# T5-bias attention followed by a three-way maxout FFN on one core: transposes moved to the PSUM banks of the attention sums, q and k loaded two batches ahead, the bias band mirrored by VectorE

## The chip, the cores and the metric

The kernel runs on one core of a Trainium2 chip (trn2). The metric is device time in microseconds (us), as the median of repeated runs. TensorE (PE) does the matrix products and transposes, VectorE (DVE) and ScalarE (ACT) read the results out of PSUM and do the elementwise work, GpSimd (POOL) issues the loads that also convert from float32 to bfloat16, and SyncE (SP) issues the plain transfers.

## The reference

Eight batches of eight heads, 576 positions, 64 numbers a head. The bias depends only on the distance between the positions, and is constant from a distance of 128 on.

```
scores = q @ k^T / 8 + bias_table[bucket(|i - j|)]
attn   = softmax(scores)
x      = (attn @ v), heads side by side          # 4608 x 512
h      = max(max(x @ w1, x @ w2), x @ w3)        # 4608 x 768
out    = h @ w_out                               # 4608 x 512
```

## The kernel before, in words

The attention runs over 32 pairs of heads: four pairs (`hp`) in each of eight batches (`b`). For a pair, q and k are transposed on TensorE (`transpose_q`, `transpose_k`, lines 333 and 343): five 128-column transposes each into one PSUM bank, then one VectorE copy to SBUF (lines 340 and 350). The scores are made with the keys on the partitions and 288 queries (`c` = 0 or 1) on the free axis. First come the scores of the last 64 keys (`et`), then four key tiles for `c` = 0 and four for `c` = 1 (`e`). Each score tile takes two PSUM banks of a pool of two such tiles, ScalarE takes the exponential (line 371), and VectorE multiplies the part near the diagonal with the exponential of the bias (lines 376 and 383, from the tiles `bandt` and `band`).

`attend` (line 394) then sums over the keys: `den` (the softmax denominator, by ones) and `o` (attention times v), with one PSUM bank each (pool `ps_a`, one buffer for each tag). ScalarE makes 1/den as exp(-ln den), and VectorE multiplies and writes `xT`, the input of the FFN. The attend steps run late: that of the previous pair's second half after the first two score tiles of `c` = 0, that of this pair's first half after the first two of `c` = 1. In the first two pairs (`keep` = 2) up to two of them are held back.

The FFN is cut into nine chunks of 512 tokens. A chunk has 72 matmuls of stage 1 (18 groups of four, each group in one bank, read out in turn by ScalarE, line 282, and VectorE, lines 285 and 288) and 24 of stage 2 (four groups of six, copied out by line 311 or 313 and stored). These 96 matmuls wait in the list `pending`. `fill(n)` issues about n of them at five places in a pair, by `RATES`; what the list doesn't hold is not carried over. A chunk enters the list when the batch that completes its tokens is done, so the first four pairs have no FFN work, and the last two chunks run after the last pair.

Before the change the transposes of the next pair take their bank from the pool `ps_f` (two banks, tag `ff`), which the FFN groups use too. `transpose_q` stands after `fill` in the first half of `c` = 0, `transpose_k` after `fill` in the second half.

TensorE runs all matmuls and transposes in the order of the program. For the other engines the builder settles the order by the dependences and its own plan; each engine works through its queue in order and waits at an instruction whose input is not there.

At the start `make_band` (line 245) builds the bias factors. A table `w_sb` of 511 exponentials for each head, symmetric about its middle, is written to DRAM and read back so that each partition has a window shifted by one (`hank`). TensorE then reverses the partitions by a product with the mirrored identity `jrev`, and VectorE copies the result from PSUM into `band`, and part of it into `bandt`. The lines that the change touches are 179 to 199 (identity, `jrev`), 212 to 225 (`w_sb`), 245 to 250 (`make_band`), 333 to 351 (transposes), 419 (`RATES`) and 424 to 461 (the loop).

Of the kernel before, what the change touches and what calls it, by code (L numbers as in the profile page):

```python
# [10 lines left out]
F32 = mybir.dt.float32  # L11
BF16 = mybir.dt.bfloat16
ALU = mybir.AluOpType
# [26 lines left out]
def kernel(  # L40
# [12 lines left out]
    nc = tc.nc  # L53
    B, H, S, D = q.shape
    d_model, d_ff = moe_w1.shape
    NB = bias_table.shape[0]
    P = 128
    assert d_model == H * D and S == 576 and D == 64 and NB == 32 and H == 8
    inv_sqrt_d = 1.0 / float(np.sqrt(D))
    HP = H // 2  # L60
# [5 lines left out]
    CH = 512  # L66
    NCH = NTOK // CH
    BAND = 3 * P
    HALF = 2 * P - 1
    WL = 2 * HALF + 1  # L70

    const = ctx.enter_context(tc.tile_pool(name="const", bufs=1))
# [16 lines left out]
    def mm(*args, **kw):  # L89
        tc.keep_in_program_order(nc.tensor.matmul(*args, **kw))  # L90
# [36 lines left out]
    def load_q(b, h0, h1, tiles):  # L127
        load_main(q, b, h0, h1, tiles[0])
        nc.gpsimd.dma_start(
            out=qtail[b % 2][0:64, h0:h1, :], in_=q[b, h0:h1, KT * P : S, :].rearrange("h p d -> p h d"),  # L130
        )

    def load_k(b, h0, h1, tiles):
        load_main(k, b, h0, h1, tiles[1])
        load_tail(k, b, h0, h1, ktail)
# [31 lines left out]
    def load_tiles():  # L167
        q_sb = loads.tile([P, KT, H, D], BF16, tag="q_sb", name="q_sb")
        k_sb = loads.tile([P, KT, H, D], BF16, tag="k_sb", name="k_sb")
        v_sb = loads.tile([P, KT, H, D], BF16, tag="v_sb", name="v_sb")  # L170
        return q_sb, k_sb, v_sb

    batch = [None] * B
# [2 lines left out]
    load_k32(2, 4)  # L176
    load_q(0, 0, 2, batch[0])

    ident_f = stage.tile([P, P], F32, name="ident_f")
    make_identity(nc, ident_f[:])  # L180
    ident = const.tile([P, P], BF16, name="ident")
    nc.vector.tensor_copy(ident[:], ident_f[:])  # L182
    load_v(0, 0, 2, batch[0])
    load_q(0, 2, H, batch[0])
    jrev_f = stage.tile([P, P], F32, name="jrev_f")
    nc.gpsimd.memset(jrev_f[:], 0.0)
    nc.gpsimd.affine_select(
        out=jrev_f[:], in_=jrev_f[:], compare_op=ALU.not_equal, fill=1.0,
        base=-(P - 1), pattern=[[1, P]], channel_multiplier=1,
    )  # L190
    jrev = const.tile([P, P], BF16, name="jrev")
    nc.vector.tensor_copy(jrev[:], jrev_f[:])
    load_v(0, 2, H, batch[0])
    ones = const.tile([P, 64], BF16, name="ones")
    nc.vector.memset(ones[:], 1.0)
# [15 lines left out]
    while ranges[single] == (single, single + 1):  # L211
        single += 1
    nc.vector.tensor_copy(w_sb[:, HALF : HALF + single], etab[:, 0:single])
    for vv, rg in enumerate(ranges):
        if rg is None or vv == NB - 1:
            continue
        lo, hi = rg
        assert hi <= P
        segs = [(HALF + lo, HALF + hi)] if vv >= single else []
        if lo > 0:  # L220
            segs.append((HALF - hi + 1, HALF - lo + 1))
        for m0, m1 in segs:
            nc.vector.tensor_copy(  # L223
                w_sb[:, m0:m1], etab[:, vv : vv + 1].to_broadcast([H, m1 - m0])
            )
# [16 lines left out]
    cast_k32(2, 4, batch[0][1])  # L242
    cast_k32(4, H, batch[0][1])

    def make_band(hp):
        for par in range(2):
            pb = ps_f.tile([P, CH], F32, tag="ff", name="pb")
            mm(pb[:, 0:BAND], lhsT=jrev[:], rhs=hank[:, 2 * hp + par, :])
            nc.vector.tensor_copy(band[hp][:, par, :], pb[:, 0:BAND])
            nc.vector.tensor_copy(bandt[hp][64 * par : 64 * par + 64, :], band[hp][0:64, par, 0:192])  # L250

    w_bf = []
    for wi, wk in enumerate((moe_w1, moe_w2, moe_w3)):
        wb = const.tile([P, DCH, d_ff], BF16, name=f"w{wi}_bf")
# [71 lines left out]
    def fill(mms):  # L326
        budget[0] = budget[0] + mms if pending else 0.0
        while pending and budget[0] >= 0.5:
            budget[0] -= 1
            pending.pop(0)()  # L330


    def transpose_q(b, hp):
        hs = slice(2 * hp, 2 * hp + 2)
        tq = ps_f.tile([P, 2 * CH], BF16, tag="ff", name="tq")
        for t in range(KT):
            tr(tq[:, P * t : P * t + P], batch[b][0][:, t, hs, :].rearrange("p h d -> p (h d)"), ident[:])
        tr(tq[:, KT * P : KT * P + P], qtail[b % 2][:, hs, :].rearrange("p h d -> p (h d)"), ident[:])
        qT = qkt.tile([P, S], BF16, tag="qT", name="qT")
        nc.vector.tensor_copy(qT[:], tq[:, 0:S])  # L340
        return qT

    def transpose_k(b, hp):
        hs = slice(2 * hp, 2 * hp + 2)
        tk = ps_f.tile([P, 2 * CH], BF16, tag="ff", name="tk")
        for t in range(KT):
            tr(tk[:, P * t : P * t + P], batch[b][1][:, t, hs, :].rearrange("p h d -> p (h d)"), ident[:])
        tr(tk[:, KT * P : KT * P + P], ktail[b % 2][:, hp, :], ident[:])
        kT = qkt.tile([P, (KT + 1) * P], BF16, tag="kT", name="kT")
        nc.vector.tensor_copy(kT[:], tk[:, 0 : (KT + 1) * P])  # L350
        return kT

    def scores(hp, qT, kT, c, t):

        sc = ps_s.tile([P, 2, CH], F32, tag="sc", name="sc")
        if c is None:
            for cc in range(2):
                mm(  # L360
                    sc[:, cc, 0:QC], lhsT=kT[:, KT * P : KT * P + P], rhs=qT[:, cc * QC : cc * QC + QC]
                )
            e = etp.tile([P, 2, QC], BF16, tag="et", name="et")
        else:
            for par in range(2):
                r = slice(64 * par, 64 * par + 64)
                mm(
                    sc[:, par, 0:QC], lhsT=kT[r, P * t : P * t + P], rhs=qT[r, c * QC : c * QC + QC]
                )
            e = ep.tile([P, 2, QC], BF16, tag="e", name="e")  # L370
        nc.scalar.activation(out=e[:], in_=sc[:, :, 0:QC], func=ACTF.Exp, scale=inv_sqrt_d)  # L371

        def factor():
            if c is None:
                lo = KT * P - P - QC
                nc.vector.tensor_tensor(
                    out=e[:, 1, lo:QC], in0=e[:, 1, lo:QC], in1=bandt[hp][:], op=ALU.mult
                )
            else:
                lo = max(P * t - P, c * QC)  # L380
                hi = min(P * t + 2 * P, c * QC + QC)
                if hi > lo:
                    nc.vector.tensor_tensor(  # L383
                        out=e[:, :, lo - c * QC : hi - c * QC], in0=e[:, :, lo - c * QC : hi - c * QC],
                        in1=band[hp][:, :, lo - P * t + P : hi - P * t + P], op=ALU.mult,
                    )

        if made:
            factor()
        else:  # L390
            factors.append(factor)
        return e
# [23 lines left out]
        nc.vector.tensor_tensor(out=xT[hp][:, x0 : x0 + QC], in0=o[:, 0:QC], in1=rd[:], op=ALU.mult)  # L416

    ready = {n: (n * CH + CH - 1) // S for n in range(NCH)}
    RATES = (6.0, 2.5, 7.0, 4.0, 4.0)
    pairs = [(b, hp) for b in range(B) for hp in range(HP)]  # L420
    late = []
    made, factors = [], []
# [1 line left out]
    for i, (b, hp) in enumerate(pairs):  # L424
        qT, kT = nxt
        ahead = pairs[i + 1] if i + 1 < len(pairs) else None
        keep = 2 if i < 2 else 0

        def behind():
            while len(late) > keep:  # L430
                late.pop(0)()

        et = scores(hp, qT, kT, None, None)
        fill(RATES[0])
        for c in range(2):
            es = []
            for half in range(2):
                for t in (2 * half, 2 * half + 1):
                    es.append(scores(hp, qT, kT, c, t))
                if half == 0:  # L440
                    behind()
                if i == 0 and c == 1 and half == 1:
                    for j in range(HP):
                        make_band(j)
                    made.append(True)
                    while factors:
                        factors.pop(0)()
                if half == 0 and c == 0 and hp == 0:
                    if b + 1 < B:
                        batch[b + 1] = load_tiles()  # L450
                        load_q(b + 1, 0, H, batch[b + 1])
                        load_k(b + 1, 0, H, batch[b + 1])
                        load_v(b + 1, 0, H, batch[b + 1])
                    for n in range(NCH):
                        if ready[n] == b - 1:
                            pending.extend(ffn_units(n))
                fill(RATES[1 + 2 * c + half])
                if ahead and c == 0 and half == 0:
                    nq = transpose_q(*ahead)
                if ahead and c == 0 and half == 1:  # L460
                    nxt = (nq, transpose_k(*ahead))
            late.append(lambda b=b, hp=hp, c=c, et=et, es=es: attend(b, hp, c, et, es))
    fill(8)
    while late:
# [37 lines left out]
```

## Time and profile before

| | |
|---|---|
| median of 3 runs | 428.99 us (428.44 to 429.12) |
| the profiled execution, its own time | 428.23 us |
| its span, first to last instruction | 426.4 us |
| TensorE busy | 385.7 us |
| VectorE busy | 248.2 us |
| ScalarE busy | 253.2 us |
| GpSimd busy | 113.6 us |
| mean granted TensorE clock | 0.998 |

Times in rows are in us from the start of the span, durations of single instructions in ns. A row of the timeline has the start, the time to the end of the last instruction of the group, the engine, the line, the operation with its output and inputs, and the count; a bracket says how long the engine was idle before it and what ended that. The end of a matmul is modelled and lies later than the start of the next one, so a short wait of TensorE does not show as idle time.

### The profile page before, as it was taken

What the parts mean: (1) busy time and instruction counts of PE and PEld (TensorE: products, weight loads), DVE (VectorE), ACT (ScalarE), POOL (GpSimd) and SP (SyncE); (2) the same over time, 40 slices, a digit from 0 to 9 for tenths busy, and PEclk for the clock granted to TensorE, in tenths of its full rate; (3) what the DMA queues carried; (4) which work ended last, traced back from release to release, by engine and by line L of the source; (5) the groups of instructions that cost most, each with busy time, mean ns of one, the idle gap of its engine ahead of it and who ended that gap; (6) DMA issues with size and microseconds to landing.
All of it is one profiled execution on the core that took longest, in us unless ns stands there. A gap on an engine that the chain in (4) does not pass through costs nothing.

```text
span 426.4 us, 7565 instructions
## 1 busy us (share of the span) xinstructions
PE 385.7 (90%) x2920; PEld 182.3 (43%) x2920; DVE 248.2 (58%) x609; ACT 253.2 (59%) x476; POOL 113.6 (27%) x149
## 2 busy tenths in 40 slices
PE   0778799889999999899999899999999998999996
PEld 0334444444444444444444444444444444444442
DVE  8583655556565665566556655566666655655352
ACT  1566967565766677667666567667666665722221
POOL 8936940524017220804052401612000000000000
PEclk9999999999999999999999999999999999999999
DMA  9999990795509380949079740919000200020202
GB/s 138 207 209 163 136 77 1 51 85 98 34 0 112 83 74 2 90 47 130 1 49 66 108 47 2 111 55 104 0 2 0 100 2 0 2 98 2 99 0 100
DMA packets 121932, 28.62 MB, mean 67 GB/s; under 512 B 113952, under 2 KB 117288, under 8 KB 121896
## 3 DMA queue, kind: packets, MB, share of 16 engines
q0 software_dynamic: 110544, 16.72, 54.2%
q1 hardware_dynamic: 11352, 11.42, 8.1%
q8 instruction: 23, 0.38, 0.4%
q14 instruction: 13, 0.11, 0.1%
HBM read 35.39 MB, written 9.45 MB: 105 GB/s over the span
## 4 chain that ended last, share of the span: by engine, by line
PE 73%; ACT 14%; DVE 10%; issue 3%; DVEq 0%
PE ps L90 38%; PE sc L90 11%; PE den L90 11%; ACT e L371 8%; PE o L90 7%; PE tk L93 3%; DVE m L285 3%; PE tq L93 2%; ACT m L282 2%; DVE hT L288 2%; ACT rd L414 2%; ACT ld L412 1%; ACT et L371 1%; DVE w_sb L223 1%; DVE xT L416 1%
## 5 line engine op out<-in xcount | busy, mean ns | idle before, releaser
L371 ACT ACTIVATE e<-sc 128x576 bf16<-128x576 f32 x256 | 152.4, 648 | 99.0 <-PE sc L90 98.8
L90 PE MATMUL ps<-xT,w_bf 128*128 128x512 bf16 x648 | 165.0, 380 | 4.9 <-ACT m L282 1.9
L383 DVE TENSOR_TENSOR e<-e,band 128x576 bf16<-128x576 bf16 (+5 forms) x224 | 78.4, 356 | 78.3 <-ACT e L371 71.7
L90 PEld LDWEIGHTS <-w_bf 128*128 128x128 bf16 x648 | 56.6, 97 | 78.7 <-issue 30.3
L90 PE MATMUL sc<-qT,kT 64*128 64x288 bf16 (+1 forms) x576 | 70.6, 295 | 6.1 <-ACT e L371 3.3
L118 POOL DMA_DIRECT2D q_sb<-in_q_dram x32 | 28.0, 898 | 104.8 <-PE sc L90 104.6
L90 PE MATMUL ps<-wo_bf,hT 128*128 128x512 bf16 x216 | 53.3, 380 | 0.0
L285 DVE TENSOR_TENSOR m<-ps,m 128x512 bf16<-128x512 f32 x54 | 37.2, 688 | 23.5 <-PE ps L90 20.8
L282 ACT ACTIVATE m<-ps 128x512 bf16<-128x512 f32 x54 | 32.3, 599 | 30.5 <-PE ps L90 30.0
L416 DVE TENSOR_TENSOR xT<-o,rd 128x288 bf16<-128x288 f32 x64 | 29.3, 457 | 32.9 <-ACT rd L414 32.9
L90 PEld LDWEIGHTS <-kT 64*128 64x128 bf16 (+1 forms) x576 | 22.4, 95 | 51.4 <-issue 37.8
L90 PE MATMUL den<-e,ones 128*64 128x288 bf16 x512 | 43.7, 293 | 0.0
L90 PE MATMUL o<-e,v_sb 128*64 128x288 bf16 x512 | 42.0, 286 | 0.0
L288 DVE TENSOR_TENSOR hT<-ps,m 128x512 bf16<-128x512 f32 x54 | 37.1, 687 | 2.8 <-PE ps L90 1.0
L90 PEld LDWEIGHTS <-ones 128*64 128x64 bf16 x512 | 23.6, 109 | 18.3 <-issue 17.1
L371 ACT ACTIVATE et<-sc 128x576 bf16<-128x576 f32 x32 | 21.0, 655 | 17.6 <-PE sc L90 15.6
L412 ACT ACTIVATE ld<-den 128x288 f32<-128x288 f32 x64 | 26.3, 412 | 7.4 <-PE den L90 7.4
L90 PEld LDWEIGHTS <-v_sb 128*64 128x64 bf16 x512 | 29.0, 110 | 2.3
L90 PEld LDWEIGHTS <-hT 128*128 128x128 bf16 x216 | 19.1, 98 | 24.6 <-issue 7.0
L414 ACT ACTIVATE rd<-ld 128x288 f32<-128x288 f32 x64 | 28.3, 442 | 2.0
L93 PE MATMUL tq<-ident,q_sb 128*128 128x128 bf16 x128 | 13.0, 227 | 17.7 <-DVE ident L182 10.8
L118 POOL DMA_DIRECT2D v_sb<-in_v_dram x32 | 28.7, 941 | 0.2 <-DMA q_sb<-in_q_dram 0.2
(53 smaller groups left out, 251.3 us busy)
## 6 DMA issues: line engine op xcount, KB each, us to landing
out_dram<-osb SPq DMA_DIRECT2D x36, 256.0 KB, 2.0
q_sb<-in_q_dram POOLq DMA_DIRECT2D x28, 128.0 KB, 4.0
k_sb<-in_k_dram POOLq DMA_DIRECT2D x28, 128.0 KB, 4.4
v_sb<-in_v_dram POOLq DMA_DIRECT2D x28, 128.0 KB, 4.9
w_bf<-in_moe_w_dram POOLq DMA_DIRECT2D x3, 768.0 KB, 10.8
k<-in_k_dram SPq DMA_DIRECT2D x8, 128.0 KB, 3.4
wo_bf<-in_moe_w_out_dram POOLq DMA_DIRECT2D x1, 768.0 KB, 16.4
hank<-w_dr SPq DMA_DIRECT2D x1, 576.0 KB, 6.1
```

The costliest lines, as they stand in the source:

```text
L90: tc.keep_in_program_order(nc.tensor.matmul(*args, **kw))
L93: tc.keep_in_program_order(nc.tensor.transpose(*args))
L118: nc.gpsimd.dma_start(out=dst[:, t, h0:h1, :], in_=x[:, t, h0:h1, :])
L223: nc.vector.tensor_copy(w_sb[:, m0:m1], etab[:, vv : vv + 1].to_broadcast([H, m1 - m0]))
L282: nc.scalar.activation(out=st["m"][:], in_=ps[:], func=ACTF.Copy)
L285: nc.vector.tensor_tensor(out=m1[:], in0=ps[:], in1=st["m"][:], op=ALU.max)
L288: nc.vector.tensor_tensor(out=hT[:, cf, :], in0=ps[:], in1=st["m"][:], op=ALU.max)
L371: nc.scalar.activation(out=e[:], in_=sc[:, :, 0:QC], func=ACTF.Exp, scale=inv_sqrt_d)
L383: nc.vector.tensor_tensor(out=e[:, :, lo - c * QC : hi - c * QC], in0=e[:, :, lo - c * QC : hi - c * QC], in1=band[hp][:, :, lo - P * t + ...
L412: nc.scalar.activation(out=ld[:], in_=den[:, 0:QC], func=ACTF.Ln)
L414: nc.scalar.activation(out=rd[:], in_=ld[:], func=ACTF.Exp, scale=-1.0)
L416: nc.vector.tensor_tensor(out=xT[hp][:, x0 : x0 + QC], in0=o[:, 0:QC], in1=rd[:], op=ALU.mult)
```

## The change

The transposes of the next pair take the banks of `ps_a`: q that of `o`, k that of `den`. Both stand directly after the `et` scores of a pair (for the first pair: after the first half of `c` = 1). The rates of `fill` are 24 a pair in place of 23.5. The loads of q and k for batch `b + 2` are issued in the last pair of batch `b`; those for batch 1 are issued before the FFN weights; v is loaded as before. `band` is read backwards along its free axis from `hank` by a VectorE copy; `jrev`, its eight matmuls and the PSUM copies are gone. The identity is made in bfloat16 at once. The mirrored small distances of `w_sb` are one reversed copy in place of 15 single ones. The factors held back in the first pair run after the first band, and the other three bands after them.

```diff
-    ident_f = stage.tile([P, P], F32, name="ident_f")
-    make_identity(nc, ident_f[:])
     ident = const.tile([P, P], BF16, name="ident")
-    nc.vector.tensor_copy(ident[:], ident_f[:])
+    make_identity(nc, ident[:])
...
-    jrev = const.tile([P, P], BF16, name="jrev")
-    nc.vector.tensor_copy(jrev[:], jrev_f[:])
...
     nc.vector.tensor_copy(w_sb[:, HALF : HALF + single], etab[:, 0:single])
+    nc.vector.tensor_copy(w_sb[:, HALF - single + 1 : HALF], etab[:, single - 1 : 0 : -1])
...
     def make_band(hp):
+        nc.vector.tensor_copy(band[hp][:], hank[:, 2 * hp : 2 * hp + 2, ::-1])
         for par in range(2):
-            pb = ps_f.tile([P, CH], F32, tag="ff", name="pb")
-            mm(pb[:, 0:BAND], lhsT=jrev[:], rhs=hank[:, 2 * hp + par, :])
-            nc.vector.tensor_copy(band[hp][:, par, :], pb[:, 0:BAND])
             nc.vector.tensor_copy(bandt[hp][64 * par : 64 * par + 64, :], band[hp][0:64, par, 0:192])
+    batch[1] = load_tiles()
+    load_q(1, 0, H, batch[1])
+    load_k(1, 0, H, batch[1])
     w_bf = []
...
-        tq = ps_f.tile([P, 2 * CH], BF16, tag="ff", name="tq")
+        tq = ps_a.tile([P, 2 * CH], BF16, tag="o", name="tq")
...
-        tk = ps_f.tile([P, 2 * CH], BF16, tag="ff", name="tk")
+        tk = ps_a.tile([P, 2 * CH], BF16, tag="den", name="tk")
...
-    RATES = (6.0, 2.5, 7.0, 4.0, 4.0)
+    RATES = (6.0, 3.0, 6.5, 4.0, 4.5)
...
         et = scores(hp, qT, kT, None, None)
+        if ahead and i > 0:
+            nxt = (transpose_q(*ahead), transpose_k(*ahead))
+        if hp == HP - 1 and b + 2 < B:
+            batch[b + 2] = load_tiles()
+            load_q(b + 2, 0, H, batch[b + 2])
+            load_k(b + 2, 0, H, batch[b + 2])
         fill(RATES[0])
...
-                if i == 0 and c == 1 and half == 1:
+                if b == 0 and c == 1 and half == 1 and hp == 0:
                     for j in range(HP):
                         make_band(j)
-                    made.append(True)
-                    while factors:
-                        factors.pop(0)()
+                        while j == 0 and factors:
+                            made.append(True)
+                            factors.pop(0)()
+                if i == 0 and c == 1 and half == 0:
+                    nxt = (transpose_q(*ahead), transpose_k(*ahead))
                 if half == 0 and c == 0 and hp == 0:
                     if b + 1 < B:
-                        batch[b + 1] = load_tiles()
-                        load_q(b + 1, 0, H, batch[b + 1])
-                        load_k(b + 1, 0, H, batch[b + 1])
                         load_v(b + 1, 0, H, batch[b + 1])
...
-                if ahead and c == 0 and half == 0:
-                    nq = transpose_q(*ahead)
-                if ahead and c == 0 and half == 1:
-                    nxt = (nq, transpose_k(*ahead))
```

## Rows read from the trace of the kernel before

**Rows 1.** The page, busy us, share of the span and instructions.

```profile
PE 385.7 (90%) x2920; PEld 182.3 (43%) x2920; DVE 248.2 (58%) x609; ACT 253.2 (59%) x476; POOL 113.6 (27%) x149
```

**Rows 2.** Groups of TensorE, 53 to 373 us: busy, mean ns, idle before, releasers.

```profile
L90 PE MATMUL ps<-xT,w_bf 128*128 128x512 bf16 x504 | 132.1, 380 | 4.9 <-ACT m L282 1.9 <-DVE hT L288 1.1 <-DVE m L285 0.8
...
L93 PE MATMUL tq<-ident,q_sb 128*128 128x128 bf16 x108 | 10.4, 218 | 6.9 <-DVE hT L288 2.7 <-DVE m L285 1.9 <-DVE osb L311 1.6
L93 PE MATMUL tk<-ident,k_sb 128*128 128x128 bf16 x108 | 10.4, 218 | 5.0 <-DVE m L285 1.9 <-DVE hT L288 1.2 <-DVE osb L311 0.8
```

**Rows 3.** Timeline of TensorE, 209 to 218 us, one pair.

```profile
209.34 0.30 PE L90 MATMUL den<-et,onesd 128*128 128x288 bf16 x1
...
210.79 1.04 PE L90 MATMUL ps<-xT,w_bf 128*128 128x512 bf16 x4
...
212.11 1.04 PE L90 MATMUL ps<-xT,w_bf 128*128 128x512 bf16 x4
212.99 0.41 PE L90 MATMUL sc<-qT,kT 128*128 128x288 bf16 x2
213.23 1.77 PE L90 MATMUL ps<-xT,w_bf 128*128 128x512 bf16 x6
214.93 0.42 PE L90 MATMUL sc<-qT,kT 64*128 64x288 bf16 x4
215.28 0.30 PE L90 MATMUL den<-et,onesd 128*128 128x288 bf16 x1
...
217.39 0.39 PE L93 MATMUL tq<-ident,q_sb 128*128 128x128 bf16 x4
...
217.76 0.42 PE L90 MATMUL sc<-qT,kT 64*128 64x288 bf16 x4
```

**Rows 4.** Timeline of TensorE: et scores of pairs 5 and 31, stage 2 after them.

```profile
61.94 0.41 PE L90 MATMUL sc<-qT,kT 128*128 128x288 bf16 x2
...
363.41 0.41 PE L90 MATMUL sc<-qT,kT 128*128 128x288 bf16 x2
...
395.72 5.34 PE L90 MATMUL ps<-wo_bf,hT 128*128 128x512 bf16 x24
```

**Rows 5.** VectorE, an FFN read-out and the k copy (groups), et factor (timeline).

```profile
L285 DVE TENSOR_TENSOR m<-ps,m 128x512 bf16<-128x512 f32 x54 | 37.2, 688 | 23.5 <-PE ps L90 20.8 <-ACT m L282 2.2
...
L350 DVE COPY kT<-tk 128x640 bf16<-128x640 bf16 x32 | 15.7, 489 | 15.3 <-PE tk L93 15.2
...
214.48 0.25 DVE L376 TENSOR_TENSOR et<-et,bandt 128x192 bf16<-128x192 bf16 x1
```

**Rows 6.** Timeline of the first 29 us, several engines.

```profile
4.01 3.46 DVE L223 COPY w_sb<-etab 8x1 bf16<-8x1 bf16 x45
7.67 0.84 DVE L163 CAST ktail<-kt 64x64 bf16<-64x64 f32 x2
10.78 0.58 PE L93 MATMUL tq<-ident,q_sb 128*128 128x128 bf16 x4 [10.78 <-DVE ident L182]
24.33 0.65 ACT L371 ACTIVATE et<-sc 128x576 bf16<-128x576 f32 x1 [5.27 <-PE sc L90]
28.10 0.42 PE L90 MATMUL den<-et,onesd 128*128 128x288 bf16 x1
```

**Rows 7.** Timeline of VectorE in `make_band`.

```profile
18.84 1.02 DVE L249 CAST band<-pb 128x384 bf16<-128x384 f32 x2 [2.00 <-PE pb L90]
19.78 0.71 DVE L250 COPY bandt<-band 64x192 bf16<-64x192 bf16 x2
...
23.20 0.43 DVE L250 COPY bandt<-band 64x192 bf16<-64x192 bf16 x2
```

**Rows 8.** Timeline of GpSimd, and the DMA issues with median us to landing.

```profile
19.56 3.52 POOL L118 DMA_DIRECT2D q_sb<-in_q_dram x4
79.29 3.50 POOL L118 DMA_DIRECT2D q_sb<-in_q_dram x4 [21.42 <-PE sc L90]
...
w_bf<-in_moe_w_dram POOLq DMA_DIRECT2D x3, 768.0 KB, 10.8
```

More of the change, by code (lines that the diff above doesn't have):

```diff
@@ L177 @@
     load_q(0, 0, 2, batch[0])
-    ident_f = stage.tile([P, P], F32, name="ident_f")
-    make_identity(nc, ident_f[:])
     ident = const.tile([P, P], BF16, name="ident")
-    nc.vector.tensor_copy(ident[:], ident_f[:])
+    make_identity(nc, ident[:])
     load_v(0, 0, 2, batch[0])
     load_q(0, 2, H, batch[0])
[L185 to L190, printed above, removed]
-    jrev = const.tile([P, P], BF16, name="jrev")
-    nc.vector.tensor_copy(jrev[:], jrev_f[:])
     load_v(0, 2, H, batch[0])
@@ L218 @@
         assert hi <= P
[L219 to L222, printed above, removed]
+        if vv < single:
+            continue
+        for m0, m1 in ((HALF + lo, HALF + hi), (HALF - hi + 1, HALF - lo + 1)):
             nc.vector.tensor_copy(
```

## The prediction, made before the changed kernel was run

> **What bounds the kernel now.** I read the busy times first: TensorE is busy for 385.7 of 426.4 us, the others for less than 60% [rows 1]. So a change is worth what it takes off TensorE's queue, and I looked for where that queue waits.
>
> In the stretch with FFN work (53 to 373 us) the groups of TensorE show idle time at three kinds of instruction only: before the q transposes 6.9 us, before the k transposes 5.0 us, before FFN stage 1 4.9 us [rows 2]. The releasers are DVE and ACT instructions that read FFN results out of the two `ff` banks (`m`, `hT`, `osb`): a transpose waits for an FFN bank. That is 11.9 of 16.8 us, or 71%.
>
> These idle times are too small, since the modelled end of a matmul hides a short gap, so I work out a floor for a pair from the starts in the timeline. One 512-column matmul behind another takes 0.216 us (24 in 5.34 us, of which 0.16 is the last one's modelled tail) [rows 4]. From rows 3: an attend step 1.45 us (209.34 to 210.79), four score matmuls 0.35 (214.93 to 215.28), the two of `et` 0.24 (212.99 to 213.23), one set of transposes 0.37 (217.39 to 217.76). A pair is 2 × 1.45 + 4 × 0.35 + 0.24 + 2 × 0.37 + 23.5 × 0.216 = 10.36 us. The measured pair is 11.60 us: 26 pairs between the first and the last `et` row, (363.41 − 61.94) / 26 [rows 4]. The shortfall is 1.24 us a pair, over 27 pairs 33 us, where 16.8 show as idle.
>
> In the first 53 us there is no FFN work. TensorE starts its transposes at 10.78 us, released by the identity's cast, and ScalarE is without work for 5.27 us up to 24.33 while the bands are made [rows 6]. These two places and the transposes are what the change touches.
>
> **The change part by part.**
>
> *Transposes in the banks of `o` and `den`.* The waits for an FFN bank before tq and tk go. Lower bound 11.9 us (the visible idle), upper bound 71% of 33, so 23 us. I take 15, nearer to the row. The work itself is the same: the ten transposes still cost 2 × 0.37 us a pair.
>
> What is late next? First the FFN groups: their own 4.9 us stay, as their chain ACT `m`, DVE `m`, DVE `hT` is untouched, and may grow as TensorE comes to it sooner. Second, a new wait: the `den` matmul of the next attend step waits until VectorE has copied kT out of its bank; behind it on TensorE's queue stand that attend step, all later scores and FFN matmuls, and ScalarE waits for those scores. Counted from the start of `et`, TensorE comes to `den` after 0.24 + 0.74 + 6 × 0.216 + 0.35 = 2.63 us. VectorE can copy qT after about 0.8 us, kT after about 1.2; the copies take 0.49 us each (qT is a little smaller) [rows 5]. If they stand behind the `et` factor, which ends 1.74 us after `et` (214.48 + 0.25 against 212.99) [rows 3, 5], kT is out at 2.7, just when it is wanted. So the price is between 0 and some 0.7 us a pair (one more FFN read-out of 0.69 us in front [rows 5]; below 0 is excluded, as a wait gives nothing). In the half-pair of rows 3 that has no transposes 14 FFN matmuls take 5.94 − 1.45 − 0.70 − 0.24 = 3.55 us against 3.02 at the floor, so even there 0.5 is lost; I do not expect that to vanish. For both I take 0.15 us a pair, 4 us in all. Net of this part: 15 − 4 = 11 us.
>
> *Rates.* 24 in place of 23.5 a pair moves 14 matmuls from behind the last pair into the pairs: 14 × 0.216 = 3 us on TensorE either way. Nothing, as TensorE is the bound in both places.
>
> *Loads of q and k two batches ahead.* GpSimd runs ahead of the program: it waited 21.42 us and issued q of batch 3 at 79.29 us, in the middle of batch 1, when the transposes had freed the buffer [rows 8]. The new place waits for the same event; its 11 issues a batch stand in the same order on GpSimd's queue (q, k, v), and the transposes, which must be the readers released for it, come a few us earlier. Nothing, either way.
>
> *Loads of batch 1 before the weights.* The three weights were issued before the q loads at 19.56 us, and one takes 10.8 us to land, so by 30.4; four q issues take 3.5 us [rows 8]. With k (four as long) and the three tails, 9 us now come in front, so the weights land by some 40 us. FFN work starts after 53 us in the old order and after some 46 in the new. Hidden, with 6 us to spare; if that cover went, the first FFN groups would wait by as much.
>
> *The start.* The identity's cast is gone, as are 15 of the 45 small copies (3.46 / 45 = 0.077 us each, 1.15 us) [rows 6]. The first k transpose then hangs on the casts that end at 8.5 us (7.67 + 0.84), or 1.15 earlier, so first scores can come 2 to 3 us earlier, if q, k and the tails have landed. In the old order TensorE and VectorE then passed the bands to and fro (5.27 us of ScalarE idle). In the new one TensorE goes on to pair 1, until the first attend step (28.10 us before [rows 6]), which needs the factors of pair 0 and, new, the banks that hold pair 2's transposes; their copies may stand behind the bands on VectorE. So VectorE's sum up to there is what counts. It loses eight PSUM casts (1.02 us for two, 4.1 in all) and gains four copies of 768 elements. The trace of before has no reversed copy. The nearest rows bound it: a `bandt` copy of 192 elements takes 0.22 us (0.43 for two) [rows 7], and at the PSUM cast's rate (1.02 us for 768) it would be 1.02. I take 0.5, so 2 us, and the gain is 2.1 (0 to 3.2). With the 1.15 us of the small copies it is 3.3; if the copies of qT and kT go in front of the bands, the whole 5.27 + 3 = 8.3 us is gained. I take 4.5, nearer to the row of VectorE's work; ends 0 and 8.3.
>
> On that copy the rows show one more thing: two `bandt` copies took 0.71 us at 19.78, while GpSimd was issuing q loads (19.56 to 23.08), and 0.43 at 23.20, when it had stopped [rows 7, 8]. The Trainium skill (SBUF — State Buffer, "SBUF: two separate sides") states that VectorE copies in a two-port mode and GpSimd's instructions shut each other out of a shared port; by it each reversed copy, unlike the PSUM casts it replaces, would pay about 0.14 us more, since the loads of batch 1 are issued just then. The Trainium skill (VectorE: DVE Perf Modes, "What auto-detection actually checks") lets steps of −1 into the fast modes, from which I estimate 0.27 us for a copy; by it the start would gain 0.9 us more, and at 0.41 with the port 0.4 more.
>
> **The sum.** −11 − 4.5 = −15.5 us against the profiled execution's own 428.23 us: 412.7. The median of the runs is 0.76 us above that execution, so the time should read 413.5.
>
> **The rivals.**
>
> *A: the wait moves.* FFN groups and transposes wait for the same two engines' read-outs; with the transposes gone from the `ff` banks TensorE runs into the next `m` or `hT` instead. For: the releasers of all three kinds of wait in rows 2 are the same instructions, and 0.5 us is lost in a half-pair without transposes. Against: with two banks for FFN alone a read-out has a whole group (0.86 us) to finish. If two thirds of the 15 come back, the steady part is 5 and the time 428.99 − 5 − 4.5 = 419.5.
>
> *B: VectorE holds `den` (the slower side).* At 2.63 us after `et` TensorE meets the copy of kT. If VectorE's queue has its factors, an FFN read-out and the `et` factor all in front, `den` is late by 0.69 us in every pair, 28 × 0.69 = 19 us, and FFN groups behind the copies wait too, so nothing of the 4.5 at the start remains either: 428.99 − 15 + 4 + 19 = 437. It decides against the change from about 0.4 us a pair ((15 − 4) / 28). For: the computed margin is about zero, and VectorE's work bunches up around `et`. Against: VectorE is idle for 42% of the span [rows 1], and the copy of kT idled 15.3 us in all for its transposes [rows 5], so it mostly came to them with an empty queue.
>
> *C: the start gives nothing,* because batch 0's q and k land no sooner than they are wanted, or the weights come late. Then 428.99 − 11 = 418.
>
> *D: more than I think:* the transposes give 23 − 4 and the start 8: 402.
>
> **How the numbers follow.** My forecast 0.52 (own range 408 to 417), A 0.18, C 0.13, B 0.07, D 0.10. The range 404 to 422 takes in A and C and most of D, and leaves out B. Within 0.2% (about 0.9 us, what a measurement of this kernel can tell from no change) would need A, B and C in a certain mixture: 0.03. Slower: B, 0.07. Faster: the rest, 0.90.
>
> **What would show it.** Right: in the steady stretch no tq or tk row waits for `m`, `hT` or `osb`, the pair takes 11.2 to 11.4 us with 24 FFN matmuls, `den` rarely waits for `kT`, and the idle before stage 1 stays under 9 us. At the start the 5.27 us hole of ScalarE is gone, the first `den` starts at 22 to 26 us and FFN begins at 47 to 51. Wrong: `den` waiting for L350 or `o` for L340 in most pairs (B); idle before `ps` well above 10 us (A); waits for DMA of `q_sb`, `w_bf` or `v_sb` on TensorE before 60 us (C). That q and k are loaded earlier than before in the steady part would contradict my reading of GpSimd's queue.

## The result, and the profile after

The changed kernel takes 415.35 us in the median of four runs (414.80 to 416.86), against 428.72 us (428.19 to 429.12): a ratio of 0.9694 (95% interval 0.9666 to 0.9723). Forecast were 413.5 us in a range of 404 to 422. The profiled execution has a span of 413.5 us, 12.9 less than before. The sum came out within 2 us, but three of its terms were wrong by more than that, in opposite directions, and the experiments show which.

TensorE's groups in the changed kernel, 53 to 360 us, in the columns of [rows 2]:

```profile
L90 PE MATMUL ps<-xT,w_bf 128*128 128x512 bf16 x504 | 130.3, 381 | 9.8 <-ACT m L274 9.8
L90 PE MATMUL den<-et,onesd 128*128 128x288 bf16 x56 | 16.6, 296 | 0.5 <-DVE kT L342 0.5
L93 PE MATMUL tk<-ident,k_sb 128*128 128x128 bf16 x104 | 10.0, 219 | 0.0
L93 PE MATMUL tq<-ident,q_sb 128*128 128x128 bf16 x104 | 10.0, 219 | 0.0
```

Against [rows 2] the idle time before tq and tk went from 6.9 and 5.0 us to nothing, and `den` almost never waits for kT. But stage 1 now idles 9.8 us in place of 4.9, all of it for one releaser, ScalarE's read-out `m`. One such place in the timeline of TensorE and ScalarE:

```profile
212.11 0.42 PE L90 MATMUL sc<-qT,kT 64*128 64x288 bf16 x4
212.45 1.19 ACT L363 ACTIVATE e<-sc 128x576 bf16<-128x576 f32 x2 [0.59 <-PE sc L90]
212.46 1.25 PE L90 MATMUL ps<-xT,w_bf 128*128 128x512 bf16 x5
213.52 0.60 ACT L274 ACTIVATE m<-ps 128x512 bf16<-128x512 f32 x1
214.18 0.59 PE L90 MATMUL ps<-xT,w_bf 128*128 128x512 bf16 x2 [0.47 <-ACT m L274]
```

Of the five FFN matmuls at 212.46 the first ends a group. Its read-out is then ready, but ScalarE has just begun two exponentials and comes to `m` at 213.52. TensorE fills the other bank and stands at 213.54 (212.46 + 5 × 0.216) before a bank that is free at 214.18, 0.64 us later; as idle time the row shows 0.47 of it. This wait comes 21 times, once in each of the 21 pairs that run stage 1 (seven chunks, three pairs each).

The start, TensorE and VectorE:

```profile
10.05 1.01 PE L90 MATMUL sc<-qT,kT 128*128 128x288 bf16 x4 [2.04 <-DVE kT L342]
20.79 0.66 PE L90 MATMUL sc<-qT,kT 128*128 128x288 bf16 x2 [4.04 <-DVE kT L342]
25.67 0.42 PE L90 MATMUL den<-et,onesd 128*128 128x288 bf16 x1
...
17.19 0.36 DVE L237 COPY band<-hank 128x768 bf16<-128x768 bf16 x1 [0.55 <-DMA hank<-w_dr]
18.60 0.63 DVE L237 COPY band<-hank 128x768 bf16<-128x768 bf16 x2
20.26 0.47 DVE L342 COPY kT<-tk 128x640 bf16<-128x640 bf16 x1
```

First scores come at 10.05 us in place of 12.59, and the first `den` at 25.67 in place of 28.10 [rows 6]. In between TensorE waits 4.04 us for the copy of pair 1's kT, since the builder put the last three bands, most of their `bandt` copies and some factors of pair 0 in front of it on VectorE. The first of these three bands (17.19) waited in turn for a part of `hank`, which comes back from DRAM only then.

How the time divides, from the starts in TensorE's timeline (FFN begins at the first stage 1 matmul; a pair is the stretch between the `et` scores of pairs 5 and 31 divided by 26):

| kernel | FFN begins | a pair | behind the last `et` | span |
|---|---|---|---|---|
| before | 53.7 | 11.60 | 63.0 | 426.4 |
| changed | 54.4 | 11.20 | 60.6 | 413.5 |
| transposes alone | 55.4 | 10.88 | 63.0 | 408.5 |
| transposes and rates | 55.8 | 11.20 | 60.1 | 414.2 |
| changed, rates 6, 4, 6, 4, 4 | 54.8 | 10.76 | 60.6 | 402.2 |

### The profile page after: what moved, and what is told of

Same layout as the page of the kernel before. It is cut to its first block, busy times and chain, and to the rows that moved or that the text cites. A ratio compares the mean times of both kernels' runs of the same rounds, so it can differ in the third digit from the quotient of the medians.

```text
span 413.5 us, 7525 instructions
## 1 busy us (share of the span) xinstructions
PE 379.2 (92%) x2912; PEld 177.9 (43%) x2912; DVE 241.4 (58%) x589; ACT 250.7 (61%) x476; POOL 113.4 (27%) x147
## 4 chain that ended last, share of the span: by engine, by line
PE 81%; ACT 10%; DMA 2%; issue 2%; DVE 2%; SPq 1%; DVEq 0%
PE ps L90 43%; PE den L90 13%; PE sc L90 11%; PE o L90 9%; ACT e L363 6%; ACT m L274 3%; PE tk L93 2%; PE tq L93 2%; DMA hank<-w_dr 2%; DMA w_dr<-w_sb 1%; SPq L154 1%; ACT rd L406 1%; ACT ld L404 1%; SPq L149 0%; DVE kT L342 0%
## 5 line engine op out<-in xcount | busy, mean ns | idle before, releaser
L90 PE MATMUL ps<-xT,w_bf 128*128 128x512 bf16 x648 | 163.2, 380 | 9.8 <-ACT m L274 9.8
L375 DVE TENSOR_TENSOR e<-e,band 128x576 bf16<-128x576 bf16 (+5 forms) x224 | 80.0, 358 | 90.6 <-ACT e L363 84.7
L90 PEld LDWEIGHTS <-w_bf 128*128 128x128 bf16 x648 | 55.4, 97 | 86.2 <-issue 38.4
L90 PE MATMUL den<-e,ones 128*64 128x288 bf16 x512 | 44.6, 297 | 0.0
L90 PE MATMUL o<-e,v_sb 128*64 128x288 bf16 x512 | 43.1, 291 | 0.0
L122 POOL DMA_DIRECT2D vtail<-in_v_dram x18 | 11.1, 626 | 82.7 <-PE o L90 77.2
L90 PEld LDWEIGHTS <-hT 128*128 128x128 bf16 x216 | 18.5, 97 | 24.3 <-issue 7.0
L363 ACT ACTIVATE et<-sc 128x576 bf16<-128x576 f32 x32 | 21.2, 663 | 11.9 <-PE sc L90 11.1
## 6 DMA issues: line engine op xcount, KB each, us to landing
w_bf<-in_moe_w_dram POOLq DMA_DIRECT2D x3, 768.0 KB, 11.4
```

Source lines behind the costliest of these rows:

```text
L122: nc.gpsimd.dma_start(out=dst[b % 2][64 * par : 64 * par + 64, h0 // 2 : h1 // 2, 64 * par : 64 * par + 64], in_=src[b, h0 + par : h1 : 2, ...
L375: nc.vector.tensor_tensor(out=e[:, :, lo - c * QC : hi - c * QC], in0=e[:, :, lo - c * QC : hi - c * QC], in1=band[hp][:, :, lo - P * t + ...
```

## The experiments

All times are medians, with the ratio to the kernel before on the same chip and, in brackets, its 95% interval.

**The transposes alone.** Edit to the kernel before:

```diff
-        tq = ps_f.tile([P, 2 * CH], BF16, tag="ff", name="tq")
+        tq = ps_a.tile([P, 2 * CH], BF16, tag="o", name="tq")
-        tk = ps_f.tile([P, 2 * CH], BF16, tag="ff", name="tk")
+        tk = ps_a.tile([P, 2 * CH], BF16, tag="den", name="tk")
         et = scores(hp, qT, kT, None, None)
+        if ahead and i > 0:
+            nxt = (transpose_q(*ahead), transpose_k(*ahead))
...
+                if i == 0 and c == 1 and half == 0:
+                    nxt = (transpose_q(*ahead), transpose_k(*ahead))
-                if ahead and c == 0 and half == 0:
-                    nq = transpose_q(*ahead)
-                if ahead and c == 0 and half == 1:
-                    nxt = (nq, transpose_k(*ahead))
```

> The kernel before with one part of the change alone: the transposes in the banks of o and den, directly behind the et scores. Old rates, old loads, bands by TensorE. Theory 1 (this part carries the gain, since FFN work starts at 54.4 us after the change and at 53.7 before it, so the start gave nothing): no wait of tq or tk for m, hT or osb, et of pair 5 to et of pair 31 in about 26 x 11.1 us, time 414 to 418 us. Rival (rates, loads or bands carry half of it): 420 us or more.

Measured: 410.90 us, ratio 0.9587 (0.9558 to 0.9616). It is 4.5 us faster than the whole change, outside both expectations. So this part is worth 18.0 us, and something else in the change costs 4.5.

**The transposes' place without their banks.** The changed kernel with `ps_f` and tag `ff` in the two lines again.

> The changed kernel with the transposes at their new place, but with their tiles taken from the two FFN banks again. Theory 1 (the bank counts, not the place): idle before tq and tk comes back to about 10 us, time 424 to 430 us. Rival (the place behind the et scores is enough, because the FFN banks are free there): at most 418 us.

Measured: 454.62 us, ratio 1.0601 (1.0580 to 1.0622), far slower than before and above both expectations. At the new place the bank decides: against the whole change the old banks cost 39 us, and the idle time before tq and tk is 8.8 and 15.6 us, more than at the old place [rows 2]. The banks of `ps_a` at the old place were not tried. TensorE and VectorE of that kernel:

```profile
213.27 0.41 PE L90 MATMUL sc<-qT,kT 128*128 128x288 bf16 x2
214.12 0.38 PE L93 MATMUL tq<-ident,q_sb 128*128 128x128 bf16 x4 [0.44 <-ACT m L274]
214.59 0.46 DVE L332 COPY qT<-tq 128x576 bf16<-128x576 bf16 x1 [0.53 <-PE tq L93]
215.10 0.38 PE L93 MATMUL tk<-ident,k_sb 128*128 128x128 bf16 x4 [0.55 <-DVE qT L332]
216.13 1.02 PE L90 MATMUL ps<-xT,w_bf 128*128 128x512 bf16 x4 [0.15 <-DVE kT L342]
```

Stage 1 of a chunk starts with the second `fill` of a pair; at the next `et` scores 3 + 7 + 4 + 4 = 18 of its matmuls are issued, four and a half groups, and the half-done group holds one of the two banks. Both transposes must then use the other in turn: tq waits for `m`, tk for the copy of qT, and the FFN for the copy of kT.

**VectorE's order at the start fixed.** Edit to the changed kernel:

```diff
-        nc.vector.tensor_copy(band[hp][:], hank[:, 2 * hp : 2 * hp + 2, ::-1])
+        ins = nc.vector.tensor_copy(band[hp][:], hank[:, 2 * hp : 2 * hp + 2, ::-1])
+        tc.keep_in_program_order(ins)
...
-                if b == 0 and c == 1 and half == 1 and hp == 0:
-                    for j in range(HP):
+                if (i, c, half) in ((0, 1, 1), (1, 0, 0)):
+                    for j in ([0] if i == 0 else [1, 2, 3]):
                         make_band(j)
-                        while j == 0 and factors:
-                            made.append(True)
-                            factors.pop(0)()
+                        made.append(j)
+                        while factors and factors[0][0] == j:
+                            factors.pop(0)[1]()
```

> The changed kernel with the order of VectorE fixed at the start: the copies of qT and kT of pair 1 in front of the first band, the other three bands behind the copies of pair 2. Theory 2 (the new order of VectorE at the start gave back what the bands had freed, 4.04 us of TensorE waiting for kT): the et scores of pair 1 start at 17 to 18 us instead of 20.8, FFN work at about 51 instead of 54.4, time 411 to 413 us. Rival (the attend steps held back in pairs 0 and 1, or the loads, set when FFN work starts): FFN work still at 54, time 414.5 to 416 us.

Measured: 414.20 us, ratio 0.9655 (0.9627 to 0.9684); 1.15 us less than the changed kernel, with intervals that overlap. The 4.04 us for kT are gone, but in its trace tq of pair 1 idles 2.36 us for the load of q (released at 17.96 us), pair 1's `et` starts at 20.25 us, and the FFN at 54.05. The time is between the two expectations, the FFN where the rival has it. Theory 2 fails: behind VectorE's order the arrival of q was nearly as late.

**Other rates.** The changed kernel with

```diff
-    RATES = (6.0, 3.0, 6.5, 4.0, 4.5)
+    RATES = (6.0, 4.0, 6.0, 4.0, 4.0)
```

> The changed kernel with the rates 6, 4, 6, 4, 4: the same 24 FFN matmuls a pair, but the first group of four ends ahead of the third and fourth score tiles, not behind them. Theory 3 (what is left is the wait of stage 1 for ScalarE's read-out, which is queued behind two exponentials: 0.64 us in 21 pairs, 13 us): the idle before stage 1 falls from 9.8 to under 3 us, the pair from 11.35 to 10.8 us, time 403 to 408 us. Rival (the wait only goes to the next read-out or to the scores): time 412 to 417 us.

Measured: 404.07 us, ratio 0.9418 (0.9400 to 0.9436), as expected; a pair takes 10.76 us. The same place in its timeline:

```profile
206.20 1.04 PE L90 MATMUL ps<-xT,w_bf 128*128 128x512 bf16 x3
207.17 0.42 PE L90 MATMUL sc<-qT,kT 64*128 64x288 bf16 x4
207.27 0.60 ACT L274 ACTIVATE m<-ps 128x512 bf16<-128x512 f32 x1 [0.57 <-PE ps L90]
207.52 1.47 PE L90 MATMUL ps<-xT,w_bf 128*128 128x512 bf16 x6
207.77 1.19 ACT L363 ACTIVATE e<-sc 128x576 bf16<-128x576 f32 x2
208.92 0.42 PE L90 MATMUL sc<-qT,kT 64*128 64x288 bf16 x4
```

The group ends ahead of the score tiles, so `m` stands in front of the exponentials, and six matmuls run without a gap. (Records of single matmuls are missing: the row of three stands for four.) Stage 1 idles 0.2 us for `m` in place of 9.8, and 4.4 us in all (53 to 350 us), where under 3 was expected. The pair is now 0.3 us above the floor of the prediction, 10.47 us with 24 matmuls (10.36 + 0.5 × 0.216).

**The rates of before in the changed kernel** (6, 2.5, 7, 4, 4):

> The changed kernel with the rates of before (6, 2.5, 7, 4, 4; 23.5 a pair in place of 24). Theory 4 (the new rates are what costs 4.4 us against the transposes alone: with exactly 24 a pair a scalar read-out falls behind two exponentials at the same place of every pair): stage 1 waits for ScalarE about 6 times in place of 21, time 410 to 412.5 us. Rival (the loads or the bands cost it): 414 to 416 us.

Measured: 411.24 us, ratio 0.9589 (0.9566 to 0.9611). Stage 1 waits for `m` 6 times, 1.8 us. The rates cost the changed kernel 4.1 us.

**Transposes and rates, without the rest:**

> The kernel before with two parts of the change: transposes, and the rates 6, 3, 6.5, 4, 4.5. Theory 4: the wait of stage 1 for ScalarE is back in some 21 pairs, 414 to 417 us. Rival: 410 to 412 us, as with the transposes alone.

Measured: 416.98 us, ratio 0.9729 (0.9713 to 0.9745). Stage 1 waits for `m` 22 times, 10.0 us; the stretch between the two `et` scores is 291.17 us, to the hundredth that of the changed kernel (352.94 − 61.77). So loads and bands do nothing in the steady part, and by the medians they and the rest of the start are worth 1.6 us, with intervals that overlap.

**The rates alone** in the kernel before:

> The kernel before with the new rates alone. My sum took the rates at nothing: 428 to 430 us. Theory 4 says that they add waits of stage 1 here too, as far as the transposes' own waits do not cover them: 429 to 436 us.

Measured: 425.76 us, ratio 0.9933 (0.9911 to 0.9955): faster, which neither side expected. Its groups from 53 us on:

```profile
L90 PE MATMUL ps<-xT,w_bf 128*128 128x512 bf16 x529 | 142.7, 380 | 13.8 <-ACT m L282 10.6 <-issue 2.4
L93 PE MATMUL tq<-ident,q_sb 128*128 128x128 bf16 x108 | 10.4, 219 | 0.0
L93 PE MATMUL tk<-ident,k_sb 128*128 128x128 bf16 x108 | 10.3, 217 | 2.8
```

The idle time is the same in all, 16.6 against 16.8 us, and so is a pair (11.58), but it holds half a matmul more, and 60.1 us are left behind the last `et` in place of 63.0. So the 14 matmuls that moved into the pairs made them no longer. The waits changed places: of the 11.9 us before the transposes [rows 2] 2.8 are left, and 10.6 stand before stage 1 for `m`. So with the old place and banks, too, the rates decide where TensorE waits. The rates 6, 4, 6, 4, 4 were not tried on the kernel before, so how much of the transposes' 18.0 us they would have brought by themselves is open.

**The loads as before** in the changed kernel:

> The changed kernel with the loads of q and k where they were (batch 1 behind the weights, the others one batch ahead in the program). My sum took them at nothing: the loads of the steady part start at the same events, time 414.5 to 416 us. Rival (the loads of batch 1 ahead of the weights delay pair 1's q or the FFN's start): 412 to 414 us.

Measured: 416.11 us, ratio 0.9708 (0.9689 to 0.9726). That is 0.1 us above the first expectation and far from the rival's; the interval overlaps that of the changed kernel, and the stretch between the two `et` scores is 291.17 us again.

**The start's parts alone** (identity, table and bands) in the kernel before:

> The kernel before with the parts of the start alone: identity made in bfloat16, reversed copies in w_sb and for the bands, nothing of the transposes, rates or loads. My sum gave this 4.5 us: 424 us. Theory 2b (what the bands free is taken back by q's arrival, VectorE's order and slow matmuls before FFN work begins): 427 to 429 us, FFN work at 53 to 54 us.

Measured: 428.20 us, ratio 0.9984 (0.9968 to 1.0001), with a wide spread (426.60 to 429.74). The trace is of the fastest of the ten runs; the FFN begins at 51.73 us there, earlier than the 53 to 54 of theory 2b. In it TensorE's transposes for pair 1 trickle in as q lands:

```profile
11.70 0.29 PE L93 MATMUL tq<-ident,q_sb 128*128 128x128 bf16 x1
12.45 0.29 PE L93 MATMUL tq<-ident,q_sb 128*128 128x128 bf16 x1 [0.45 <-DMA q_sb<-in_q_dram]
13.90 0.29 PE L93 MATMUL tq<-ident,q_sb 128*128 128x128 bf16 x1 [1.17 <-DMA q_sb<-in_q_dram]
15.12 0.29 PE L93 MATMUL tq<-ident,q_sb 128*128 128x128 bf16 x1 [0.93 <-DMA q_sb<-in_q_dram]
17.07 0.29 PE L93 MATMUL tq<-ident,qtail 128*128 128x128 bf16 x1 [1.67 <-DMA qtail<-in_q_dram]
```

**Old start, moved transposes, rates 6, 4, 6, 4, 4:**

> The kernel before with the transposes moved and the rates 6, 4, 6, 4, 4, old loads and bands. If the start is worth nothing: 403 to 405.5 us, as the changed kernel with these rates (404.1). If the start is worth my 4.5 us: 408 us or more.

Measured: 404.99 us, ratio 0.9445 (0.9431 to 0.9459), 0.9 us above the kernel with the new start and loads, with intervals that overlap. In this order of VectorE the start is worth one us or nothing.

**Both edits, rates and VectorE's order:**

> The changed kernel with both edits, rates 6, 4, 6, 4, 4 and the fixed order of VectorE at the start. If the two add (11.3 and 1.1 us): 403 us; if the start's 1 us is noise: 404 us.

Measured: 402.25 us, ratio 0.9385 (0.9369 to 0.9400). This is the fastest version, 13.1 us below the changed kernel; the two edits add. Its FFN begins at 52.5 us. Against the kernel with the old start and the same rates (404.99) it is 2.7 us faster, and here the intervals are apart: with VectorE's order fixed the new start and loads bring 2.7 us, still less than the 4.5 of the prediction.

**Fewer attend steps held back** (`keep` is 1 in the first four pairs) on top of it:

> As the kernel with both edits, but at most one attend step is held back in the first four pairs, in place of two in the first two. Theory 2c (three attend steps in a row in pair 2, each waiting for the one o bank, leave ScalarE without work for 4 us): FFN work starts at 50 to 52 us in place of 54, time 400 to 402 us. Rival (q's arrival and slow matmuls set the start): 403 to 404.5 us.

Measured: 403.59 us, ratio 0.9411 (0.9397 to 0.9425). Theory 2c fails: FFN work begins at 54.9 us, against 52.5 in the kernel that it started from. The steps no longer come three in a row, but two now stand together in pair 4 ahead of the FFN, and TensorE's clock fell on the way (last section).

## Why the prediction was right, and where three terms failed

*Which wait goes:* right in the place, wrong in the size. The idle time before tq and tk is gone, and the transposes alone bring 18.0 us. I took 15 less 4 given back, so 11; the stretch between the `et` scores fell by 18.5 us with that part alone (301.5 to 283.0). The estimate of 15 was too near to the visible idle of 11.9 (the upper bound was 23), and next to nothing of the 4 was given back.

*The new wait for kT (rival B):* wrong as a danger with FFN work, right without it. In the steady part `den` comes 2.55 us after `et` (2.63 was my sum), but VectorE copies qT before the `et` factor, not behind it, so kT is out at 2.03 to 2.33 us and not at 2.7; `den` idles 0.5 us in all. One pair of the changed kernel with the rates 6, 4, 6, 4, 4, where order and times are the same, TensorE and VectorE:

```profile
212.92 0.41 PE L90 MATMUL sc<-qT,kT 128*128 128x288 bf16 x2
213.65 0.46 DVE L332 COPY qT<-tq 128x576 bf16<-128x576 bf16 x1
214.29 0.26 DVE L368 TENSOR_TENSOR et<-et,bandt 128x192 bf16<-128x192 bf16 x1 [0.19 <-ACT et L363]
214.47 0.48 DVE L342 COPY kT<-tk 128x640 bf16<-128x640 bf16 x1
215.47 0.30 PE L90 MATMUL den<-et,onesd 128*128 128x288 bf16 x1
```

In the first pairs, where no FFN matmuls stand between, the wait shows; the transposes-alone kernel at 44 us:

```profile
44.51 0.39 PE L93 MATMUL tk<-ident,k_sb 128*128 128x128 bf16 x4
44.88 0.55 PE L90 MATMUL sc<-qT,kT 64*128 64x288 bf16 x4
45.95 0.28 PE L90 MATMUL den<-et,onesd 128*128 128x288 bf16 x1 [0.53 <-DVE kT L350]
```

Three such waits of 0.53 us stand in the first pairs of that kernel (at 33.41, 45.95 and 53.77 us), and its FFN begins 1.7 us later than before (55.4).

*Rates at nothing:* this step failed. I counted matmuls and not where a group ends. In the change, with exactly 24 a pair, six groups of four, the same group falls behind the same two exponentials in every stage 1 pair, and the idle time before stage 1 is 9.8 us, where I had named under 9; with 23.5 the place drifts, and stage 1 waited for `m` 6 times in the transposes-alone kernel. The price is 0.32 us a pair (11.20 against 10.88), 8.2 us over 26, less 2.4 to 2.9 behind the last pair: some 5.5, and 4.1 to 6.1 by the medians. It isn't the number 24 that costs: 6, 4, 6, 4, 4 is 24 too. On the kernel before the same rates gain 3.0. Rival A had named the mechanism (TensorE runs into the next read-out), but its cause is the rates and not the move.

*The start at 4.5:* this step failed. Alone it is worth 0.6 us (0 to 1.4 by its interval), and together with the loads and VectorE's order fixed 2.7. The FFN begins 0.7 us later than before, not 3 to 7 us earlier: the 5.27 us hole of [rows 6] went, and behind it stood in turn kT's copy (4.04 us, an order that I had named as a risk), the landing of `hank` (up to 17.19 us) and of q (the last transpose of pair 1's q starts at 15.33 us in the changed kernel and at 17 to 18 in others), and `den` waiting for kT. How much each takes was not tried for `hank` and q. Rival C, which let the start give nothing because q lands no sooner than it is wanted, named one of these; I gave it too little.

*The reversed copy:* 0.36 us each (0.35 to 0.36 for all four), below the 0.5 I took and above the 0.27 of the estimate. The Trainium skill (VectorE: DVE Perf Modes, "What auto-detection actually checks") lets a step of −1 into the fast modes; the trace is in line with that, since a forward `bandt` copy of 192 elements takes 0.20 us undisturbed and the reversed 768 take only 0.16 more. The same copy forwards stands in no run. Of the exclusive port that VectorE and GpSimd share by the Trainium skill (SBUF — State Buffer, "SBUF: two separate sides") these copies show nothing: the one at 18.60 us ran while GpSimd issued nothing, the one at 14.69 us while it did, and they took the same time (0.36). The 0.14 us more for each that the prediction worked out did not come.

*Loads:* right. q of batch 3 is issued at 74.05 us, when the k transposes in pair 6 end:

```profile
74.05 3.53 POOL L118 DMA_DIRECT2D q_sb<-in_q_dram  x4 [14.09 <-PE tk L93]
```

The event is the one of [rows 8], the transposes of pair 7 that free the buffer, which both kernels do in pair 6. It comes 5.2 us earlier because they stand earlier in the pair: the q transposes start 0.25 us after that pair's `et` (73.11), and 5.1 us after it before (78.61 against 73.52). The weights' last wait on GpSimd ended at 39.10 us, where 40 was expected.

So the steady part with its end gave 12.7 us (10.3 and 2.4) where I had 11, and all up to the `et` scores of pair 5 gave 0.2 where I had 4.5. The nearness of the sum is luck: the transposes brought 7 us more than I took, the rates ate some 5.5 that I had at nothing, and the start brought some 4 less. The pair of 11.20 us, too, lies in the 11.2 to 11.4 that I had named only because a larger gain (to 10.88) and an unforeseen loss (0.32) met there.

## What to carry to other kernels

A transpose or other short use of PSUM that shared a rotation with long accumulations cost more here than its visible wait (18.0 us against 11.9), and far more where a half-done group held one of the two banks (454.62 us); look for a bank whose owner is idle at that moment. When work is dealt out in fixed portions between other stages, see where a group ends against the queue of the engine that reads it out: end it ahead of the long instructions, and don't let the pattern repeat on the bad place. A stall that goes at the start shows the next latest input, so list the landing times of all inputs first.

## What the runs showed of the hardware that was not expected

At the start matmuls run at about half their later rate. In the changed kernel the same eight `den` matmuls take 1.17 us at 26.27 and 32.35 us, and 0.68 at 35.32; from the first of them to the `o` matmuls behind it is 0.96 us at 26.27 and 0.51 at 35.32. The last two rows are of the kernel before.

```profile
26.27 1.17 PE L90 MATMUL den<-e,ones 128*64 128x288 bf16 x8
32.35 1.17 PE L90 MATMUL den<-e,ones 128*64 128x288 bf16 x8
35.32 0.68 PE L90 MATMUL den<-e,ones 128*64 128x288 bf16 x8
...
28.69 0.83 PE L90 MATMUL den<-e,ones 128*64 128x288 bf16 x8
29.36 0.66 PE L90 MATMUL o<-e,v_sb 128*64 128x288 bf16 x8
```

The kernel before comes to the full rate within the eight at 28.69 us, the changed kernel only between 32.35 and 35.32, some 5 us later; no term of the prediction has that. The granted clock is recorded as 1.00 in both; what makes them slow is not shown in these traces. In the kernel with fewer steps held back the record has the same slowness as a fall of the clock in the middle of the start. Columns: stretch, its length, TensorE busy, granted clock, DMA share, GB/s.

```profile
26.50:31.00 4.50, 2.99 (x33) 1.00 1.50 138
31.00:33.00 2.00, 0.82 (x10) 1.00 1.14 209
33.00:34.20 1.20, 0.67 (x11) 0.79 1.17 207
34.20:37.00 2.80, 2.80 (x20) 0.50 1.16 210
37.00:39.00 2.00, 1.14 (x10) 0.98 1.16 210
```

TensorE had been busy for 0.82 of 2 us, then the clock fell to 0.50 of full speed (1.2 of 2.4 GHz), and it came back after 2.8 us without a gap. The eight matmuls took 1.17 us there (at 34.74) against 0.68 at 28.78 and 39.08. While the clock is low each such group costs 0.5 us more. That may be one reason why holes closed at the start brought so little; it was not tried by itself.
